# Rebuilding the convolution part of an S4 + MLP kernel: factored kernel tables in four channel chunks and a shifted 2048-point transform

## The chip, the cores and the metric

One core of one Trainium2 chip. The metric is the device time of one execution in microseconds. A *span* is the part of an execution that the profile covers; it is about 2 us shorter than the time.

Names of engines in the profile: PE is the TensorE matmul, PEld its weight load, DVE is VectorE, ACT is ScalarE, POOL is GpSimd, SP is SyncE (here it only issues DMA). `L88` is line 88 of the kernel that the line belongs to.

## The reference, cut to what matters

```python
def _A_ref(u, A_re, A_im, B_re, B_im, C_re, C_im, log_dt, Dskip):   # S4 convolution
    dt = exp(log_dt)[:, None]                    # D = 512 channels, N = 128 modes, L = 2048
    logdA = dt * (A_re + 1j * A_im)
    l = arange(L).astype(A_re.dtype)             # bfloat16: the time index is ROUNDED
    P = exp(logdA[:, :, None] * l)
    K = einsum("dn,dnl,dn->dl", C, P, dt * B).real
    y = irfft(rfft(pad(u)) * rfft(pad(K)))[:L]   # linear convolution by a 4096-point FFT
    return y + u * Dskip

h   = x + _A_ref(layernorm(x), ...)
out = h + mlp(layernorm(layernorm(h)))           # 512 -> 1376 -> 512, gelu
```

Two facts matter. The kernel `K` needs exponentials of 128 modes at 2048 times for 512 channels, which is done by products of small tables and a sum over modes on PE. And the time index is cast to bfloat16, which has 8 significant bits, so above 256 most indices coincide.

## The kernel before: the parts that matter

The tables of decay and phase are made for 256 channels at a time, twice. A table has 64 columns on one side (`P0`, 33 to -31) and 32 on the other (`Q1`, itself 4 x 8 products). POOL makes the arguments, ACT the exponentials and sines, DVE the products. POOL uses `tensor_scalar`:

```python
def trig_batch(nc, sc, pc, c2, js, halfpi):                 # 256 channels, 4 indices at a time
    for jj, j in enumerate(js):
        nc.gpsimd.tensor_scalar(Y[:, jj, :], psi_c, float(j), MAGIC, ALU.mult, ALU.add)
    nc.gpsimd.tensor_scalar(Q[:, :J, :], Y[:, :J, :], 1.0, -MAGIC, ALU.mult, ALU.add)
    for jj, j in enumerate(js):
        nc.vector.scalar_tensor_tensor(F[:, jj, :], psi_c, float(j), Q[:, jj, :], ALU.mult, ALU.subtract)
    ...                                                     # ACT: |F|, sin, cos
# exp_batch: nc.gpsimd.tensor_scalar(TH[:, jj, :], th_c, float(j), 0.0, ALU.mult, ALU.add), then ACT exp

for c2 in range(2):                                         # two halves of the channels, in turn
    tabs = gen_tables(nc, tb, sc, q1p, pc, c2, halfpi)
    kgen_matmuls(nc, kps_pool, tabs, c2, K_old)             # sum over modes: 512 small matmuls
k_to_tl(nc, tc, K_old, K_sb, identb)                        # permute
```

Then the transform of `K` goes through DRAM once, and the frequency loop takes 33 frequencies, with PSUM operands on DVE:

```python
for f1 in order:                                            # phase_u_main
    nc.tensor.matmul(X[:],  lhsT=Tall[:, f1, 64:192], rhs=B_all[:, f1, :], ...)
    nc.tensor.matmul(Xs[:], lhsT=Tall[:, f1, 0:128],  rhs=B_all[:, f1, :], ...)
    nc.vector.tensor_tensor(P1[:], X[:],  KF[:, f1, :], ALU.mult)
    nc.vector.tensor_tensor(P2[:], Xs[:], KF[:, f1, :], ALU.mult)
    ...                                                     # two matmuls to zp, ACT copies it to Z_sb
```

After it, Z goes to DRAM and comes back transposed (`ZT`), and the MLP follows, with `y2` on ACT in one block and a 16 us POOL addition of the bias b2.

## Time and profile before

| | us |
|---|---|
| time, median (four runs) | 587.77 (587.32 to 588.07) |
| start to first generation matmul | 159.9 |
| from there to ZT landed | 298.9 |
| ZT landed to the end of the span | 126 |

The page of the kernel before; first the busy time of each engine, then the busy tenths of 40 equal slices of the span (so one digit is 14.6 us):

```profile
span 584.6 us, 5246 instructions
PE 222.6 (38%) x1777; PEld 113.1 (19%) x1789; DVE 371.1 (63%) x600; ACT 249.9 (43%) x298; POOL 232.5 (40%) x259
...
PE   2004300000087000003966063299400501999997
DVE  6789897599969959996358166499508562200222
POOL 2930159887780899553782245400000000900000
```

No engine is full over the span, but PE has long rows of zeros where DVE and POOL read mostly 7 to 9 (5 at the least): PE waits for tables. The windows view of the kernel before gives the same by stage (columns: stretch, length, busy time and number of instructions of each engine, granted PE clock, DMA share, GB/s):

```profile
core 0: us, PE busy (x) PEld busy (x) DVE busy (x) ACT busy (x) POOL busy (x), PEclk, DMA share, GB/s
85.00:160.00 75.00, 0.10 (x4) 0.13 (x7) 63.36 (x88) 43.79 (x43) 62.99 (x89) 1.00 0.02 6
160.00:296.00 136.00, 47.72 (x1024) 46.83 (x1024) 104.18 (x140) 71.82 (x56) 87.34 (x77) 0.69 0.00 1
376.00:418.00 42.00, 38.28 (x125) 10.68 (x128) 39.74 (x66) 19.31 (x34) 0.62 (x1) 0.94 0.19 79
418.00:459.00 41.00, 0.00 (x0) 0.02 (x1) 13.12 (x2) 0.00 (x0) 1.84 (x3) 0.51 0.94 235
```

The groups of the page (line, engine, operation, out<-in, shape, count; then busy us and mean ns; then the idle time before them and what ended most of it) name the wait, 181.5 us of it, and the two instructions that fill POOL and DVE:

```profile
L198 PE MATMUL kps<-P0r,Q1r 128*32 128x64 bf16 x512 | 47.4, 389 | 184.7 <-DVE P0r L186 181.5
L86 POOL TENSOR_SCALAR TH<-th 128x256 f32<-128x256 f32 x86 | 66.2, 773 | 25.6 <-ACT P0r L91 10.8
L103 DVE SCALAR_TENSOR_TENSOR F<-psi,Q 128x256 f32<-128x256 f32 x86 | 50.5, 633 | 20.2 <-POOL Q L100 20.2
```

The chain of waits of the kernel before shows the 41 us in which only DMA runs (columns: start, length, what):

```profile
417.68 11.60 DMA Z_dram<-Z_sb
...
430.29 25.57 DMA ZT<-Z_dram
...
455.88 2.89 DMA ZT<-Z_dram
```

### The profile page before, as it was taken

Reading aid. Unit: us, or ns where it says so; the run is one execution under the profiler, and the core shown is the slowest. Engines: PE = TensorE matmul, PEld = TensorE weight load, DVE = VectorE, ACT = ScalarE, POOL = GpSimd, SP = SyncE. Lnnn points to the kernel's source line nnn. Section 1 sums busy time; section 2 is a strip of 40 time slices with the busy share of each in tenths; the row PEclk is TensorE's granted clock in tenths of the full one; section 3 lists DMA queues with packets and bytes.
Section 4 is the critical chain, followed back from the end, with each engine's and each line's share of the span. In section 5 each row is a group of like instructions: output and inputs, shape, how many; then the busy total and the mean of one; then the engine's idle time right before and its main releaser. Section 6 shows DMA issues by size and latency. Waiting matters only on the chain. (4 is left out here: it accounts for less than half of the span.)

```text
span 584.6 us, 5246 instructions
## 1 busy us (share of the span) xinstructions
PE 222.6 (38%) x1777; PEld 113.1 (19%) x1789; DVE 371.1 (63%) x600; ACT 249.9 (43%) x298; POOL 232.5 (40%) x259
## 2 busy tenths in 40 slices
PE   2004300000087000003966063299400501999997
PEld 1000000000086000003931010022100100544443
DVE  6789897599969959996358166499508562200222
ACT  3345335746699543463147141344200007777100
POOL 2930159887780899553782245400000000900000
PEclk9999999999999555555975567599855655899999
DMA  2412890000000000000071990021599170000122
GB/s 63 108 40 108 330 286 0 0 0 0 0 3 1 1 0 0 0 0 1 3 284 77 311 205 0 0 82 72 163 319 230 21 203 1 0 1 0 38 55 54
DMA packets 23307, 44.72 MB, mean 76 GB/s; under 512 B 6848, under 2 KB 19648, under 8 KB 21104
## 3 DMA queue, kind: packets, MB, share of 16 engines
q1 hardware_dynamic: 13408, 23.27, 13.0%
q10 hardware_dynamic: 8112, 12.10, 7.5%
q0 software_dynamic: 1760, 9.01, 4.7%
q8 instruction: 14, 0.23, 0.2%
q14 instruction: 13, 0.11, 0.1%
HBM read 27.40 MB, written 21.23 MB: 83 GB/s over the span
## 5 line engine op out<-in xcount | busy, mean ns | idle before, releaser
L198 PE MATMUL kps<-P0r,Q1r 128*32 128x64 bf16 x512 | 47.4, 389 | 184.7 <-DVE P0r L186 181.5
L86 POOL TENSOR_SCALAR TH<-th 128x256 f32<-128x256 f32 x86 | 66.2, 773 | 25.6 <-ACT P0r L91 10.8
L198 PEld LDWEIGHTS <-Q1r 128*32 128x32 bf16 x512 | 36.4, 179 | 182.3 <-issue 96.9
L103 DVE SCALAR_TENSOR_TENSOR F<-psi,Q 128x256 f32<-128x256 f32 x86 | 50.5, 633 | 20.2 <-POOL Q L100 20.2
L105 ACT ACTIVATE AF<-F 128x1024 f32<-128x1024 f32 (+1 forms) x22 | 30.6, 1390 | 58.6 <-DVE F L103 58.6
L98 POOL TENSOR_SCALAR Y<-psi 128x256 f32<-128x256 f32 x86 | 51.3, 601 | 5.3 <-ACT P0r L91 0.3
L532 DVE TENSOR_TENSOR ot<-o2ps,h_sb 128x512 bf16<-128x512 f32 x16 | 11.1, 691 | 63.9 <-PE o2ps L530 61.8
L199 PE MATMUL kps<-P0i,nQ1i 128*32 128x64 bf16 x512 | 47.3, 385 | 0.0
L100 POOL TENSOR_SCALAR Q<-Y 128x1024 f32<-128x1024 f32 (+1 forms) x22 | 34.5, 1568 | 17.0 <-DVE F L103 16.1
L523 PE MATMUL h1ps<-y2T,w_sb 128*128 128x512 bf16 (+1 forms) x171 | 40.5, 379 | 0.6 <-ACT hT L525 0.3
L530 PE MATMUL o2ps<-w_sb,hT 128*128 128x512 bf16 (+1 forms) x173 | 38.2, 379 | 0.2
L199 PEld LDWEIGHTS <-nQ1i 128*32 128x32 bf16 x512 | 36.7, 181 | 3.7 <-issue 3.7
L510 POOL TENSOR_TENSOR h_sb<-h_sb,b_b 128x8192 f32<-128x8192 f32 x1 | 15.7, 15727 | 49.4 <-ACT y_3293 L509 49.4
L525 ACT ACTIVATE hT<-h1ps,b_sb 128x512 bf16<-128x512 f32 (+1 forms) x44 | 30.1, 688 | 8.8 <-PE h1ps L523 8.8
L108 ACT ACTIVATE S<-F 128x1024 bf16<-128x1024 f32 (+1 forms) x22 | 30.7, 1394 | 0.1
L445 ACT CAST Z_sb<-zps 128x512 bf16<-128x512 f32 x33 | 19.2, 586 | 22.4 <-PE zps L444 22.4
L376 PE MATMUL u_aps<-u_sb,BD_108 64*128 64x512 bf16 x32 | 10.8, 590 | 45.1 <-DVE u_sb L421 40.8
L109 ACT ACTIVATE C<-AF,halfpi 128x1024 bf16<-128x1024 f32 (+1 forms) x22 | 26.3, 1194 | 0.0
L89 ACT ACTIVATE P0r<-TH 128x1024 bf16<-128x1024 f32 (+1 forms) x16 | 16.4, 1025 | 20.6 <-POOL TH L86 20.5
L406 ACT ACT_TABLE_LOAD x2 | 2.6, 1283 | 51.4 <-DVE h_sb L483 51.4
L482 PE MATMUL yps<-ZT,Dmat 128*64 128x512 bf16 x32 | 7.4, 514 | 43.2 <-DMA ZT<-Z_dram 42.0
L364 DVE CAST KF<-kfps 128x512 bf16<-128x512 f32 x17 | 11.0, 685 | 17.5 <-PE kfps L396 17.4
(346 smaller groups left out, 662.4 us busy)
## 6 DMA issues: line engine op xcount, KB each, us to landing
B_all<-Bt_dram SPq DMA_DIRECT2D x1, 4224.0 KB, 13.7
H_dram<-u_sb POOLq DMA_DIRECT2D x1, 2048.0 KB, 6.8
A_dram<-u_A SPq DMA_DIRECT2D x2, 1024.0 KB, 5.6
AK_dram<-k_A SPq DMA_DIRECT2D x2, 1024.0 KB, 4.8
Z_dram<-Z_sb SPq DMA_DIRECT2D x2, 1024.0 KB, 7.7
u_sb_3146<-H_dram SPq DMA_DIRECT2D x1, 2048.0 KB, 19.8
Bt_dram<-A_dram SPq DMA_DIRECT2D x6, 256.0 KB, 10.6
KF<-AK_dram SPq DMA_DIRECT2D x6, 256.0 KB, 12.8
```

The source lines that it names most:

```text
L86: nc.gpsimd.tensor_scalar(TH[:, jj, :], th_c, float(j), 0.0, ALU.mult, ALU.add)
L98: nc.gpsimd.tensor_scalar(Y[:, jj, :], psi_c, float(j), MAGIC, ALU.mult, ALU.add)
L100: nc.gpsimd.tensor_scalar(Q[:, :J, :], Y[:, :J, :], 1.0, -MAGIC, ALU.mult, ALU.add)
L103: nc.vector.scalar_tensor_tensor(F[:, jj, :], psi_c, float(j), Q[:, jj, :], ALU.mult, ALU.subtract)
L105: nc.scalar.activation(AF[:, :J, :], F[:, :J, :], ACT.Abs)
L108: nc.scalar.activation(S[:, :J, :], F[:, :J, :], ACT.Sin, scale=S2PI)
L109: nc.scalar.activation(C[:, :J, :], AF[:, :J, :], ACT.Sin, scale=-S2PI, bias=halfpi[:])
L198: nc.tensor.matmul(o, lhsT=Q1r[:, :, cc], rhs=P0r[:, :, cc], start=True, stop=False, tile_position=(0, 32 * g))
L199: nc.tensor.matmul(o, lhsT=nQ1i[:, :, cc], rhs=P0i[:, :, cc], start=False, stop=True, tile_position=(0, 32 * g))
L523: nc.tensor.matmul(pt[:fs, :], lhsT=w1_sb[:, dc, fc * P:fc * P + fs], rhs=y2T[:, dc, 4 * tb:4 * tb + 4, :], start=(dc == 0), stop=(dc == 3))
L525: nc.scalar.activation(hT[:fs, fc, 512 * tb:512 * tb + 512], pt[:fs, :], ACT.Gelu_apprx_tanh, bias=b1_sb[:fs, fc:fc + 1], scale=1.0)
L530: nc.tensor.matmul(pt[:], lhsT=hT[:fs, fc, j * P:(j + 1) * P], rhs=w2_sb[:fs, fc, :], start=(fc == 0), stop=(fc == NFC - 1))
```

## The change

Its intent is to do less table work and to overlap it.

- The bfloat16 rounding is used: the 2048 times have only 20 x 33 distinct parts that need a table. The factor C·B goes into the small table as a magnitude `G` and an angle `gam`, so there are no products to build it. 96 planes and 28 products become 53 planes.
- Phases are 32-bit integers, where a left shift does the wrap-around, in place of adding and subtracting a large constant.
- A 4096-point transform with 33 frequency groups becomes a quarter-shifted 2048-point one with 32, whose spectra are kept in bfloat16 in SBUF. A product then is one DVE instruction of 1024 columns. The second product needs the spectrum with its halves exchanged (`KFs`), which is made by DMA.
- The filter's work runs in four chunks of 128 channels; chunk c+1's tables are meant to fill the gaps of chunk c.
- In the tail, `y2` is pipelined on DVE by tile and b2 is a 97th row of w2.

The diff, cut to its core (constants, loads, and the `u` side are left out):

```diff
-JB = 4
-def trig_batch(...):            # 256 columns, POOL: mult+add
-        nc.gpsimd.tensor_scalar(Y[:, jj, :], psi_c, float(j), MAGIC, ALU.mult, ALU.add)
+def gen_tables(nc, tb, sc, pc, ch, halfpi):        # 128 columns, POOL: mult alone
+    for k0, n in [(1, 8), (9, 8)]:
+        for e in range(n):
+            gp.tensor_scalar(TH[:, e, :], thc, float(8 * (k0 + e)), None, ALU.mult)             # L287
+        act.activation(Br[:, 16 + k0:16 + k0 + n, :], TH[:, :n, :], ACT.Exp)
+        act.activation(Br[:, neg(k0, n), :], TH[:, :n, :], ACT.Exp, scale=-1.0)
+    for a0, n in [(0, 7), (7, 7), (14, 6)]:
+        for e in range(n):
+            gp.tensor_scalar(TH[:, e, :], thc, float(lA[a0 + e]), None, ALU.mult)               # L293
+        ...
+    for k0, n in [(1, 8), (9, 8)]:
+        for e in range(n):
+            gp.tensor_scalar(cod[:, e, :], psic, float(8 * (k0 + e) * 2 ** 24), None, ALU.mult) # L307
+        v.tensor_scalar(cod[:, :n, :], cod[:, :n, :], 8, None, ALU.logical_shift_left)          # L308
+        C, S = trig(cod, n, 1.0)
+        ...                                         # four DVE products; the same for Ar, Ai (L318 to L323)
+    for ch in range(4):
+        tabs = gen_tables(nc, tb, sc, pc, ch, halfpi)
+        kgen(nc, kpss, ch, tabs, Kg, ev)            # "generation": 256 small matmuls (L338, L339)
+        k_stage1(nc, mm, W, Kg, AK, ev)             # 128 small matmuls (L366)
+        nc.sync.dma_start(AK_dram[ch][:], AK[:])
+        for q in range(4):                          # read back transposed: pieces of 256 bytes
+            dqs[q % 2].dma_start(KF[32 * q:32 * q + 32], AK_dram[ch][32 * q:32 * q + 32].rearrange("f s d -> s f d"))
+        ...                                         # 32 matmuls, evicted to KF (L470)
+        nc.sync.dma_start(KFs[0:64], KF[64:128])    # L473
+        nc.scalar.dma_start(KFs[64:128], KF[0:64])
+        for f8 in range(0, 32, 8):
+            v.tensor_tensor(KF[:, f8:f8 + 8, :], KF[:, f8:f8 + 8, :], X[:, f8:f8 + 8, cs], ALU.mult)
+            v.tensor_tensor(KFs[:, f8:f8 + 8, :], KFs[:, f8:f8 + 8, :], X[:, f8:f8 + 8, cs], ALU.mult)
+            ...                                     # 16 matmuls, evicted to Z (L482, L483)
+        nc.sync.dma_start(Z_dram[ch][:], Z[:])
+    tables.close()                                  # only now is there room for w1, w2, b1, h, ZT
+    ...                                             # loads of w1, w2, b1 (2-byte pieces); L505 casts b1 on DVE
+    for ch in range(4):
+        for q in range(4):
+            dqs[q % 2].dma_start(ZT[32 * q:32 * q + 32, :, CW * ch:CW * ch + CW], Z_dram[ch]...)  # L511
```

The names in a chunk: `Kg` is the generated kernel, `AK` its first transform stage, `KF` its spectrum (made by the "filter matmuls", L470), `Z` the product with the spectrum of `u` after the inverse stage, `ZT` the same read back transposed.

## The prediction

> **What bounds it now.** No engine is full (page: DVE 371 of 585 us, ACT 250, POOL 233, PE 223); stages run in turn.
> - To 160 us: constants, layer norm, u transform, tables of 256 channels. From 85 to 160 (windows) DVE and POOL are busy 63 us each; in the waits the generation matmuls wait 181.5 us for DVE's table products.
> - 160 to 296: generation, second tables (208-290: DVE 62 us), generation.
> - 296 to 376: permute, FFT stage 1, DRAM round trip (PE idle 15.6 us), TP tables.
> - 376 to 418: frequency loop, DVE 95% busy on 66 PSUM products of 0.68 us.
> - 418 to 459: Z to DRAM and back alone: the chain has 11.6+25.6+2.9 us.
> - 459 to 585: h, layer norm (9.0 us for the b2 load), y2 on ACT (11.4 us), MLP 84 us.
>
> **Removed, added, moved.** Tables fall from 96 planes x 512 channels, plus 28 products, to 53 planes. POOL goes from about 205 us in table stages to 208 instructions of 128 columns, by estimate 60 us (256 columns took 399 ns at best), so DVE escapes contention (its 256-column F: 360 ns at best, 609 median). Permute and Xs matmuls go; 66 products become 32 bf16 ones of 1024 (0.60-0.68 us). But each of four chunks has a chain: generation (256 matmuls at 45 ns, 12 us), 128 small stage-1 matmuls, eviction, DRAM write and read-back in 256-byte pieces, 32 matmuls, half-swap DMA, products, 64 matmuls, Z write. Table work fills the gaps only partly: in program order DVE's last products of chunk c+1 stand behind the KF evictions of chunk c, so generation c+1 waits for chunk c's DRAM trip.
>
> **Sum (estimates from those durations).**
> - Start to first generation: DVE about 11 +20 (phase of C·B, W) +19 (T codes, statistics) +26 (u, evictions, skip) +5 TP +27 tables +10 X evictions = 118, plus waits 18: 137 us (160 before).
> - Chunk period: 48, 53, 53 us: generation, Z and stage 1 about 28, eviction 2, write 6, read 9, KF 6, rest waits. Generation of chunk 3 starts at 291.
> - Its drain is exposed: 28+2+6+9+10 (KF, half-swap) +13 (products, Z) +13 (Z write, last ZT quarter) = 81, plus 20 because w1, w2, h and three ZT quarters (8 MB) are issued just then. ZT complete near 392.
> - Tail 116 us instead of 126: y2 pipelined, no b2 wait.
>
> Together about 508 profiled. Some contention may hide: **500 us**, range **455 to 545**. Faster by over 2% 0.95, within 2% 0.03, slower 0.02.
>
> The Trainium skill, "DMA: Bandwidth & Descriptors" (Specifications), puts line rate at 512 bytes and more; the read-backs go from 1024 to 256 bytes. Before loaded 128 KB in such pieces in 2.3-3.0 us. "ScalarE: Activation LUTs" gives 1283 ns per table load; before shows that, 16 times; after has 21.
>
> **Right or wrong.** Right if first generation starts at 120-155 us; four periods of 45-60 us with DVE idle before the Kg and KF evictions; POOL under 90 us, DVE near 300; last ZT to end 110-120; TensorE waits for KF from DRAM in every chunk. Wrong if POOL still paces tables or PE is busy throughout.
>
> **What would make it wrong.** 256-byte reads far slower than 9 us per MB (+10 us per chunk makes 540); int32 shifts or reciprocal on DVE slow; half clock on PE (granted in 190-370); or better overlap, DVE-bound chunks of 40 us, giving 455.

## The result, and the profile after

Ratios here and below are the mean time of one kernel's fast runs over that of the other's of the same rounds, so they are not quite the ratios of the medians quoted.

| | before | after | predicted |
|---|---|---|---|
| time, median us (four runs each) | 587.77 | 479.03 (477.30 to 479.82) | 500 (455 to 545) |
| ratio, 95% interval | | 0.8148 (0.8129 to 0.8166) | |
| span, us | 584.6 | 477.8 | "about 508 profiled" |
| start to first generation | 159.9 | 134.4 | 137 |
| first to last generation | | 146.1 (49.9 + 48.9 + 47.3) | 154 (48 + 53 + 53) |
| last generation to ZT landed | | 85.4 | 101 |
| first generation to ZT landed | 298.9 | 231.5 | 255 |
| ZT landed to end | 126 | 112 | 116 |

The gain of 107 us in the span is thus 25.5 at the start, 67.4 in the middle and 14 in the tail.

The same parts of the page, of the kernel after (one digit is 11.9 us):

```profile
span 477.8 us, 6704 instructions
PE 203.9 (43%) x2576; PEld 128.4 (27%) x2584; DVE 263.4 (55%) x550; ACT 207.3 (43%) x257; POOL 135.2 (28%) x292
...
PE   2000033501641306630673056401252549999996
DVE  7289999980931765777487746210352983021022
POOL 5991740000399239923984000000010000000000
```

DVE lost 108 us and POOL 97. From the twelfth to the twenty-fourth digit (134 to 281 us) PE, DVE and POOL alternate: each chunk is visible as one bump. The windows of the kernel after, for the first wait, the chunk loop up to the last generation, the drain (from the last generation until ZT has landed) and the tail (columns as before):

```profile
85.00:134.00 49.00, 15.76 (x162) 9.05 (x160) 34.70 (x68) 25.20 (x39) 6.87 (x11) 0.72 0.63 150
134.00:281.00 147.00, 56.41 (x1404) 49.23 (x1408) 94.25 (x179) 93.44 (x109) 82.74 (x150) 0.58 0.31 73
281.00:366.00 85.00, 26.17 (x531) 23.17 (x520) 23.82 (x36) 11.07 (x17) 1.84 (x2) 0.60 0.83 182
366.00:478.00 112.00, 92.63 (x440) 42.61 (x448) 40.84 (x90) 31.73 (x33) 0.00 (x0) 0.86 0.08 19
```

In the loop no engine is busy for more than about 94 of 147 us, so no single engine bounds it; that a serial chain does is argued here and tested by e5_notab below. The granted PE clock in it is 0.58; what that adds to the chain was not tested. The groups show what POOL does (64 + 80 + 64 = 208 instructions, 121.9 us together, where the prediction had 60):

```profile
L287 POOL TENSOR_SCALAR TH<-th 128x128 f32<-128x128 f32 x64 | 38.4, 600 | 99.0 <-ACT S L301 90.2
L293 POOL TENSOR_SCALAR TH<-th 128x128 f32<-128x128 f32 x80 | 45.3, 594 | 3.0 <-ACT Br L289 1.8
L307 POOL TENSOR_SCALAR codb<-psi 128x128 int32<-128x128 f32 x64 | 38.2, 597 | 10.9 <-ACT Ar L294 4.2
```

They have half the columns of the ones in the kernel before, and take nearly as long. The view of waits of the kernel after names who waits (columns: engine, line, releaser; total us, number, longest):

```profile
DVE codb L308 <- POOL codb L307: 19.1, 5, 10.0
PE kfps L470 <- DMA KF<-AK_dram_62: 17.5, 1, 17.5
DVE b_sb L505 <- DMA b_bf<-in_B_b_dram: 11.7, 1, 11.7
ACT AK L86 <- DMA w_sb<-in_B_w_dram: 10.0, 1, 10.0
```

PE waits for KF from DRAM in each chunk (17.5, 17.4, 19.6 and 27.4 us). And the chain of waits of the kernel after, at the start of the last generation (`kps`), shows the predicted order: DVE's last table products (`Ai`, `Ar`) stand between and behind the KF evictions of the chunk before, and PE starts generation just after the last of them:

```profile
277.62 0.69 DVE KF L88
278.31 0.47 DVE Ai L322
278.77 0.58 DVE KF L88
...
279.93 0.56 DVE Ar L323
280.54 0.27 PE kps_90 L338 x4
```

Then the drain, in the same chain:

```profile
300.27 13.64 DMA b_bf<-in_B_b_dram
...
315.41 8.05 DMA AK_dram_65<-AK
...
323.93 9.08 DMA KF<-AK_dram_65
...
337.64 7.15 DMA KFs<-KF
...
353.46 4.26 DMA Z_dram_69<-Z
...
358.12 7.75 DMA ZT<-Z_dram_69
```

Stage 1 is done at 305.9, but its evictions are held by two loads that the engines reach first in program order: DVE casts b1 when its 2-byte pieces have landed (313.9), and ACT's queue waits for w2 (to 312.0). These two waits are called the walls below. The write of AK starts at 315.4 and takes 8.05 us, where those of the other chunks took 3.8 to 3.9.

### The profile page after: what moved, and what is told of

The parts are those of the page before. It is cut to its first block, busy times and chain, and to the rows that moved or that the text cites. A ratio compares the mean times of both kernels' runs of the same rounds, so it can differ in the third digit from the quotient of the medians.

```text
span 477.8 us, 6704 instructions
## 1 busy us (share of the span) xinstructions
PE 203.9 (43%) x2576; PEld 128.4 (27%) x2584; DVE 263.4 (55%) x550; ACT 207.3 (43%) x257; POOL 135.2 (28%) x292
## 5 line engine op out<-in xcount | busy, mean ns | idle before, releaser
L287 POOL TENSOR_SCALAR TH<-th 128x128 f32<-128x128 f32 x64 | 38.4, 600 | 99.0 <-ACT S L301 90.2
L470 PE MATMUL kfps<-KF,T 128*128 128x128 bf16 x128 | 14.3, 310 | 81.9 <-DMA KF<-AK_dram_65 27.4
L293 POOL TENSOR_SCALAR TH<-th 128x128 f32<-128x128 f32 x80 | 45.3, 594 | 3.0 <-ACT Br L289 1.8
L559 DVE TENSOR_TENSOR ot<-o2ps,h_sb 128x512 bf16<-128x512 f32 x16 | 11.1, 692 | 61.2 <-PE o2ps L557 42.6
L307 POOL TENSOR_SCALAR codb<-psi 128x128 int32<-128x128 f32 x64 | 38.2, 597 | 10.9 <-ACT Ar L294 4.2
L551 ACT ACTIVATE hT<-h1ps,b_sb 128x1024 bf16<-128x1024 f32 (+1 forms) x22 | 24.5, 1114 | 31.0 <-PE h1ps L549 30.9
L470 PEld LDWEIGHTS <-T 128*128 128x128 bf16 x128 | 13.3, 146 | 83.7 <-issue 83.7
L366 PE MATMUL k1ps<-Kg,W 20*128 20x256 bf16 (+1 forms) x512 | 23.1, 325 | 24.1 <-DVE AK L88 12.0
L482 PE MATMUL zps<-KF,TP_94 128*128 128x128 bf16 x128 | 24.9, 285 | 16.4 <-DVE KF L477 16.4
L366 PEld LDWEIGHTS <-W 20*128 20x128 bf16 x512 | 17.7, 117 | 28.0 <-issue 23.4
L483 PE MATMUL zps<-KFs,TP_95 128*128 128x128 bf16 x128 | 23.3, 282 | 2.7 <-DVE KFs L478 2.6
L557 PEld LDWEIGHTS <-hT 128*128 128x128 bf16 (+1 forms) x176 | 17.2, 98 | 20.8
L549 PEld LDWEIGHTS <-w_sb 128*128 128x128 bf16 (+1 forms) x176 | 17.5, 101 | 18.8 <-issue 0.2
L482 PEld LDWEIGHTS <-TP_94 128*128 128x128 bf16 x128 | 15.9, 131 | 20.9 <-DVE KF L477 16.5
L302 ACT ACTIVATE C<-AB,halfpi 128x1024 bf16<-128x1024 f32 (+2 forms) x20 | 21.1, 1055 | 0.3 <-ACT S L301 0.3
## 6 DMA issues: line engine op xcount, KB each, us to landing
X<-AU_dram ACTq DMA_DIRECT2D x2, 1024.0 KB, 19.6
```

The lines of the kernel that those rows point to most:

```text
L287: gp.tensor_scalar(TH[:, e, :], thc, float(8 * (k0 + e)), None, ALU.mult)
L293: gp.tensor_scalar(TH[:, e, :], thc, float(lA[a0 + e]), None, ALU.mult)
L302: act.activation(C[:, :n, :], AB[:, :n, :], ACT.Sin, scale=-SINSC, bias=halfpi[:])
L307: gp.tensor_scalar(cod[:, e, :], psic, float(8 * (k0 + e) * 2 ** 24), None, ALU.mult)
L366: nc.tensor.matmul(o, lhsT=W[rows, v, tl, :], rhs=r, start=(n == 0), stop=(n == len(js) - 1), tile_position=(32 * g, 0))
L470: nc.tensor.matmul(pt[:, k, :], lhsT=T[:, f0 + k, :], rhs=KF[:, f0 + k, :], start=True, stop=True)
```

## The experiments

The theory (A in most expectations): the sum of the prediction was right in its terms, and what is left to gain lies in two waits that the trace of the kernel after shows, POOL's slow table instructions and the two walls in the drain, so that taking each away gives about its length. The main rival (B): behind each wait lies another of nearly the same length, a serial chain in the loop and contention for DMA in the drain, so that taking one away moves the time little.

Twelve kernels ran. Each was timed in rounds with the kernel before on the same chip, whose median stayed between 587.8 and 588.9. The rounds ran on three chips and the kernel after was not timed again in them, so a difference from it, or between runs of different rounds, holds such a difference of rounds too. Stage times are those of each run's own trace. An edit is against the kernel after unless it says otherwise.

### What did the removed table work and the tail cost before?

**b1_notab**, against the kernel before; the second set of tables is not built (wrong, relative error 0.047).

```diff
-                        tabs = gen_tables(nc, tb, sc, q1p, pc, c2, halfpi)
+                        if c2 == 0:
+                            tabs = gen_tables(nc, tb, sc, q1p, pc, c2, halfpi)
```

> The kernel before, wrong result on purpose: the second set of tables (256 channels) is not built, the first is used twice. In the trace of before the second generation starts about 103 us after the first ends. Theory A, this table work lies wholly on the path: 95 to 110 us less, 478 to 493 us. Theory B, something else fills that gap: less than 60 us.

Measured: 490.90 us (ratio 0.8333, 0.8315 to 0.8350), 98 us less, in the range of theory A. The second set lay on the chain with nearly its whole length: before, the change had 98 us to gain there alone.

**b2_tail**, against the kernel before; the changed tail's `y2` by tile on DVE, and b2 as a row of w2.

```diff
+        nc.scalar.dma_start(w2_sb[96:97, 10, :], b2.rearrange("(o d) -> o d", o=1))
-        for j in range(16):
-            nc.scalar.activation(y2[:, j, :], h_sb[:, j, :], ACT.Identity, bias=nmr[:, j:j + 1], scale=rstd[:, j:j + 1])
-        nc.gpsimd.tensor_tensor(h_sb[:], h_sb[:], b2_b[:].unsqueeze(1).to_broadcast([P, 16, 512]), ALU.add)
+            nc.vector.tensor_scalar(y2[:], h_sb[:, j, :], rstd[:, j:j + 1], nmr[:, j:j + 1], ALU.mult, ALU.add)
```

> The kernel before with one part of the change alone: the second normalisation is applied on DVE tile by tile ahead of each transpose instead of 16 ACT passes first, and b2 comes as a 97th row of the last w2 block instead of a POOL addition. The pass on ACT took 11.4 us on the chain. Theory A: 6 to 11 us less, 577 to 582 us. Theory B, the MLP matmuls already hide it: within 2 us.

Measured: 577.48 us (ratio 0.9806, 0.9780 to 0.9831, so about the 2% line), 11.4 us less, as in theory A. That is most of the 14 us that the tail gained; the first MLP matmul starts at about 490 in place of 500 us.

### What do the tables cost after the change?

**e5_notab**: tables for chunk 0 alone (wrong, relative error 0.057).

```diff
-        tabs = gen_tables(nc, tb, sc, pc, ch, halfpi)
+        if ch == 0:
+            tabs = gen_tables(nc, tb, sc, pc, ch, halfpi)
```

> Wrong result on purpose: tables are built for chunk 0 only and reused by chunks 1 to 3, so all other work, the DRAM trips included, stays. Theory A, the tables (POOL codes first, DVE products last) set most of the period of 48 us: periods fall to 25 to 35 us and the time by 45 to 75 us, 405 to 435 us. Theory B, the chain through DRAM sets the period whatever the tables cost: at most 20 us less.

Measured: 445.37 us (ratio 0.7559), 33.7 us less. Both ranges were missed. The four generations now run close behind one another (from 136.8; all but the last 80 of 1,024 matmuls by 181.4 us, those at 194 to 196), but the filter matmuls still start at 168.7, 212.7, 259.8 and 303.1, a period of 43 to 47 us against 47 to 57 of the kernel after. So most of a period is not tables. It is a chain in series: filter matmuls, eviction, half-swap DMA, products, Z matmuls, then stage 1 of the next chunk (PE takes it in program order behind Z), its eviction, AK to DRAM and back. The run has a flaw of its own: without tables the MLP loads are released at about 195 us and stretch this very chain. In its trace the second KF read took 13.4 us and the half-swap after it 10.3, and the load of b1 entered the chain for 5.1; in the kernel after such a read takes 7.4 and a swap about 7. The last two AK writes took 9.0 each, where the kernel after had 3.9 in mid-loop. From this trace, first filter matmul to next AK write is 23.7 us; with 4.0 us for the write and the 7.4 us that the read takes in the kernel after, an undisturbed chain is about 35 us, an estimate. The other 12 to 15 us of a period would then be waits for tables. Together with b1_notab it shows how the large gain came about: a second table set cost 98 us before, and three sets after cost 34 us.

### Is POOL's table work the wait that is left?

**e3_twoop**: the three POOL lines take the two-operation form that the kernel before had, with a second operation that does nothing.

```diff
-            gp.tensor_scalar(TH[:, e, :], thc, float(8 * (k0 + e)), None, ALU.mult)
+            gp.tensor_scalar(TH[:, e, :], thc, float(8 * (k0 + e)), 0.0, ALU.mult, ALU.add)
(the same for the two other lines)
```

> The 208 POOL multiplications of 128 columns took 527 ns at best, while the kernel before had 399 ns at best for 256 columns with a multiply and an add. Only the form is changed: multiply and add zero. Theory A, the form with one operation is the slow one: 128 columns take 200 to 300 ns, POOL busy falls from 135 to 70-85 us, and the time by 6 to 14 us, as DVE waited 19.1 us for POOL's codes. Theory B, a fixed cost per instruction or contention with DVE: POOL stays at 130 to 140 us, time unchanged.

Measured: 462.52 us (ratio 0.7879, 0.7858 to 0.7900), 16.5 us less than the kernel after, correct, and the best correct kernel. That is theory A, and slightly past its ranges (6 to 14 us, and POOL busy 70 to 85 us). The view by line shows it; first the kernel after, then e3 (columns: number, then ns min/median/max, first and last start, shape):

```profile
L287 POOL TENSOR_SCALAR TH<-th x64: 527/528/1219, 9.9 to 232.3; 128x128 f32<-128x128 f32 x64
```

```profile
L287 POOL TENSOR_SCALAR TH<-th x64: 297/298/833, 10.5 to 217.8; 128x128 f32<-128x128 f32 x64
```

Adding an operation makes the instruction faster, 528 to 298 ns (medians). At 298 ns each the 208 instructions would make 62 us, close to the prediction's 60; in e3's trace they are busy 77.0 us, as their mean is above the median (371 to 397 ns by line, the longest 833). POOL is busy 90.7 us in place of 135.2, next to the predicted "under 90". DVE's wait for the codes, 19.1 us in the kernel after, is now:

```profile
DVE codb L308 <- POOL codb L307: 6.0, 4, 2.0
```

Generations start at 133.2, 172.7, 221.9 and 265.9; the first period fell by 10.4 us, about the 10 us that DVE waited for POOL in chunk 0 of the kernel after while AK evictions stood behind it. By stage the span's 17.3 us are 1.2 at the start, 13.4 in the periods, 2.6 in the drain and 0.1 in the tail. Why the one-operation form is slow was not tested: no run varied anything but the second operation, so the cause inside POOL stays open.

### Does another program order free the loop?

**e6_pipe**: the back half of chunk c (filter matmuls, swap, products, Z) is emitted after stage 1 of chunk c+1, so that PE's stage 1 no longer stands behind Z.

```diff
-    for ch in range(NCH):
+    def front(ch):      # tables, generation, stage 1, AK to DRAM and back
+        ...
+        return KF
+    def back(ch, KF):   # filter matmuls, swap, products, Z
+        ...
+    for ch in range(NCH + 1):
+        if ch < NCH: KFq[ch] = front(ch)
+        if ch > 0:   back(ch - 1, KFq[ch - 1])
```

> Source order only: the second half of chunk c (KF matmuls to Z) is written after the tables, generation and stage 1 of chunk c+1, so that generation c+1 no longer stands behind chunk c's trip through DRAM. Theory A, the in-order trip sets the period of 48 to 50 us: periods near 40 us, PE's waits for KF nearly gone, 15 to 25 us less, 455 to 464 us. Theory B, the table work itself or POOL sets it: period 46 to 50, within 5 us of the changed kernel.

Measured: 500.40 us (ratio 0.8516), 21 us slower. Generations start at 136.7, 180.7, 244.9 and 309.6. DVE waits 46.7 us for POOL's codes in the loop in place of 19.1 overall, up to 17.7 us at one place (line below), with an eviction behind it that PE needs: the new order puts DVE's next tables ahead of evictions, and POOL is slow at them. Both theories missed.

```profile
DVE codb L308 <- POOL codb L307: 46.7, 6, 17.7
```

**e8_twoop_pipe**: e6 and e3 together.

> e3_twoop with the source order of e6_pipe. e6_pipe alone was 21 us slower: POOL's codes, 527 ns each, came 17.7 us late in front of DVE's evictions. Theory A, with POOL at 298 ns the order now pays: 10 to 25 us less than e3_twoop, 438 to 453 us. Theory B, the trip through DRAM was never what set the period, and the order only lengthens the drain: 463 us or more.

Measured: 465.26 us (ratio 0.7893), 35 us faster than e6 but no better than e3 (the intervals of the ratios overlap). Theory B has the number (463 us or more) and not the reason: the drain is 5.5 us shorter than e3's (77.3 us) and the three periods together 6.9 us longer (139.6). DVE's wait for codes is down to 18.3 us, so the slow POOL form was the cause of e6's loss; what remains is that DVE stands 36.6 us (four times, up to 11.6) ahead of products for the half-swap DMA, as it had in e6 (37.4 us). Generations: 133.1, 166.9, 219.5, 272.7. The wait moved from PE's stage 1 to the swap.

```profile
DVE codb L308 <- POOL codb L307: 18.3, 6, 7.6
DVE KF L480 <- DMA KFs<-KF: 36.6, 4, 11.6
```

**e10_twoop_swapmm**: e3, with the half-swap made by PE: 64 more matmuls with the halves of T exchanged, evicted straight to KFs, and no DMA.

```diff
+            pw = mm.tile([P, 4, CW], f32, name="kfsps", tag="mm")
+                for r in range(2):
+                    nc.tensor.matmul(pw[64 * r:64 * r + 64, k, :], lhsT=T[:, f0 + k, 64 - 64 * r:128 - 64 * r], rhs=KF[:, f0 + k, :], ..., tile_position=(0, 64 * r))
-        nc.sync.dma_start(KFs[0:64], KF[64:128])
-        nc.scalar.dma_start(KFs[64:128], KF[0:64])
```

> e3_twoop, and the half-swapped KF spectrum comes from 64 small matmuls with the two halves of T exchanged, evicted straight into KFs, instead of two SBUF-to-SBUF DMAs after the eviction. With no tables at all the period stayed near 45 us, so a serial chain sets it: KF matmuls, half-swap DMA (6.9-7.2 us on the chain of e3_twoop), products, Z, stage 1 of the next chunk, DRAM trip. Theory A, that chain: 3 to 6 us less per chunk net of the added matmuls and evictions, 12 to 24 us in all, 439 to 451 us. Theory B, generation in program order hides the DMA except in the last chunk: at most 7 us less.

Measured: 483.96 us (ratio 0.8228), 21 us slower than e3. Both missed. The filter phase of chunk 0 takes 13.1 us in place of 3.7, and PE is busy in all of it, at a granted clock of 0.50. It saves about 7 us of DMA wait and costs 9.4 us, and generation of the next chunk, which in e3 had run during the swap and ended at 178.3 us, now mostly comes after the filter phase and ends at 195.6.

**e11_all3**: e10 with the order of e6.

> e10_twoop_swapmm with the source order of e6_pipe as well (second half of chunk c after stage 1 of chunk c+1). In e8_twoop_pipe the periods were 34, 53 and 53 us, with DVE idle 9 to 12 us before the products, on the half-swap DMA, in the middle of the next tables. Theory A, chain by DMA: with the half-swap DMA gone nothing on DVE or PE waits for a DMA in mid-chunk, periods fall to 36 to 42 us, 10 to 25 us less than e10_twoop_swapmm. Theory B, DVE's work (tables, products and evictions, about 45 us a chunk) is the next limit: within 8 us of e10_twoop_swapmm.

Measured: 466.82 us (ratio 0.7934), again no better than e3 (4.3 us more). That is 17 us less than e10, in theory A's range, but the periods are 33.8, 54.9 and 55.5 us and not 36 to 42, so its reason missed; theory B missed. e3, e8 and e11 take away different waits of the trace and end within 5 us of each other, which suggests that the loop has several chains of nearly the same length; no run shows that directly.

### Do the 256-byte pieces cost much?

**e4_contig**: KF is read in plain order, in pieces of 8 KB (wrong, relative error 0.021).

```diff
-            dqs[q % 2].dma_start(KF[...], AK_dram[ch][32 * q:32 * q + 32].rearrange("f s d -> s f d"))
+            dqs[q % 2].dma_start(KF[...], AK_dram[ch][32 * q:32 * q + 32])
```

> Wrong result on purpose: the changed kernel with the filter read KF taken from AK in plain order, so in pieces of 8 KB instead of 256 bytes. Theory A (the small pieces are a real cost of cutting to 128 channels): the read's time on the chain falls from 7.4 to 9.1 us to about 4, in each of the four chunks, and as it lies on the serial chain, the total falls by 8 to 16 us from the changed kernel's 479.0, to 463 to 471 us. Theory B (the read is bound by latency and by other transfers, or its time is hidden behind the next tables): at most 4 us less, 475 us or more.

Measured: 474.62 us (ratio 0.8046), 4.4 us less by the medians and 6 by the ratios; between the two ranges, nearer to B. A quarter (256 KB) lands in 3.2 us on SP's queue and 5.2 on ACT's, against 4.7 and 6.4 (medians of the first three chunks), so small pieces cost 1.2 to 1.5 us and not the half of the read. The filter matmuls of the four chunks start 0.5, 0.9, 1.1 and 3.9 us earlier; this run's first generation started 1.9 us later (136.3), so from there it is 2.4, 2.8, 3.0 and 5.8 us. The saving thus shows in the first chunk and the last, while the second and third add only 0.4 and 0.2; that tables hide it there is likely, not shown.

### What do the walls and the company in the drain cost?

**e1_b1cast**: the cast of b1 goes from DVE to POOL.

```diff
-    v.tensor_copy(b1_sb[:], b1_bf[:])
+    nc.gpsimd.tensor_copy(b1_sb[:], b1_bf[:])
```

> Only the cast of the b1 bias moves from DVE to POOL. In the drain of the last chunk DVE stands 11.7 us before this cast and ACT stands 10.0 us before its own stage-1 evictions (for the w2 load), both until 312-314 us. Theory A, two walls in parallel: taking one away gives at most 3 us, about 476 us. Theory B, the DVE wait is what costs: about 11 us less, 468 us.

Measured: 477.77 us (475.02 to 481.44), ratio 0.8136 (0.8092 to 0.8179): no difference that shows, as theory A said. DVE's wall is gone, but ACT still waits 10.0 us for w2 with the other half of the evictions behind it. AK is written 33.9 us after the last generation starts, against 34.9. Two waits run in parallel and end within 2 us of each other, so removing one of them gives almost nothing.

**e2_poolissue**: e1, and the loads of w1, w2, b1, b2, h and the first three chunks' ZT are issued by POOL, so neither DVE nor ACT nor their queues stand behind them.

```diff
-    nc.sync.dma_start(w1_sb[:], ...)
+    nc.gpsimd.dma_start(w1_sb[:], ...)
(the same for w2, b1, b2, h, and for ZT where ch < 3)
```

> As e1_b1cast, and w1, w2, b1, b2, h and the first three quarters of ZT are issued from POOL, idle at that point, so no DMA issue stands in the streams of ACT and SP before the evictions and copies of the last chunk. The bytes are the same. Theory A, in-order waits at issue: 10 to 16 us less than the changed kernel, 463 to 469 us. Theory B, the extra 20 us are contention for bandwidth: at most 3 us less.

Measured: 485.55 us (ratio 0.8272), 6.5 us slower than the kernel after; theory A missed, and contention (theory B) did more than cancel the gain. The chain of waits of e2:

```profile
306.51 11.61 DMA AK_dram<-AK
...
318.53 22.80 DMA KF<-AK_dram
```

The write starts 9 us earlier, as intended, and then takes 11.6 us in place of 8.05, and the read 22.8 in place of 9.1: the transfers that matter share the 16 DMA engines with 8 MB that do not. The traces bear this out: during the read the DMA engines moved 156 GB/s in e2 and 153 in the kernel after, so the rate was the same, but 3.56 MB in place of 1.46 went by, of which KF is 1. The Trainium skill, "DMA: Bandwidth & Descriptors" (Rules for kernel authors), says that spreading DMAs over issuing engines does not help bandwidth because all use the same 16 engines; this run agrees. In the kernel after, the walls had held the write back until w1, w2 and h had landed (312.2 us), and SP and ACT issued the twelve ZT pieces spread over 298 to 338 us; in e2 POOL issued all twelve at 311 to 324, on top of the read. In that sense the old order had worked as a brake.

**e12_held**: e3, with b1 loaded in the first phase, the other loads issued by POOL, and those of h and of the first three chunks' ZT held until the last KF has landed, by a one-column copy that needs KF.

```diff
+        if ch == NCH - 1:
+            nc.gpsimd.tensor_copy(hold[:], KF[:, 0, 0:1])
+        if ch < NCH - 1:
+            nc.gpsimd.tensor_copy(ZT[:, 0, CW * ch:CW * ch + 1], hold[:])
-            dqs[q % 2].dma_start(ZT[...], Z_dram[ch]...)
+            (nc.gpsimd if ch < NCH - 1 else dqs[q % 2]).dma_start(ZT[...], Z_dram[ch]...)
(the same hold for h; w1, w2 from gpsimd; b1 load and cast with the first phase's loads)
```

> The POOL two-operation form as in e3, and in addition the drain between the last generation and the last transposed read is relieved: the bias b1 is loaded in the first phase, its cast and all reads of w1, w2, h and of the transposed Z of the first three chunks are issued by POOL, and those of h and Z are held back (by a one-column copy that needs the last chunk's spectrum) until the last chunk's filter read has landed. Theory A (in e3 the last chunk's write of AK and its read of KF are slow, 8.2 and 9.2 us, and start about 11 us late because DVE and ACT stand behind bulk loads; take both the walls and the company away): AK write about 4 us, KF read 7 to 8 us, written from about 287 us instead of 298, the last ZT lands at 333 to 339 instead of 349, total 447 to 453 us. Theory B (company only moves: the held 5 MB then slow the half-swap, the Z write and the last ZT read as much as was gained): ZT lands at 345 or later, total within 4 us of e3's 462.5, or slower.

Measured: 469.33 us (ratio 0.7955, 0.7921 to 0.7989), some 5 us slower than e3 by the ratios and 7 by the medians; the profiled run was the slowest of the four, at 471.65. Two things happened. First, a fault of the edit: the scheduler put b1's cast at the front of POOL's program, where POOL waited 8.0 us for the load in 2-byte pieces, so all came late (first generation at 143.5 us, not 133.2). Second, the drain itself, from last generation to ZT landed, took 82.6 us against 82.8 in e3. The chains of waits of e3, then of e12:

```profile
298.20 8.16 DMA AK_dram<-AK
...
306.83 9.15 DMA KF<-AK_dram
...
320.60 7.20 DMA KFs<-KF
...
336.16 4.23 DMA Z_dram<-Z
```

```profile
302.47 3.86 DMA AK_dram<-AK
...
306.74 8.12 DMA KF<-AK_dram
...
319.48 12.53 DMA KFs<-KF
...
340.65 10.03 DMA Z_dram<-Z
```

The write and the read are 5.3 us shorter and AK is written 6 us sooner after generation (26.1 us, not 32.3), but the swap and the Z write are 11.1 us longer. That is theory B: the company moved. The drain has to bring in about 8 MB for which memory is free only when the tables are closed. Whether fewer bytes there, or room made earlier, would gain was not tried.

## Why the prediction was right, and where it was not

The time, 479.03 us, lies in the range, and the direction was nearly sure. The sum was 30 us too long (508 against a span of 477.8), and lowering it to 500 "as some contention may hide" had no ground. Point by point:

1. **Tables were the bound, and their removal the gain.** Right. b1_notab puts 98 us on one table set before; e5_notab puts 34 us on three sets after. What the shorter transform gave by itself was not run. The start (137 predicted, 134.4 measured), the tail (116, 112) and the first period (48, 49.9) came out close; the start in part by luck, as DVE was busy 104.8 us of it and not 118, and idle 29.6 and not 18. Over the whole span DVE was busy 263.4 us, not "near 300".
2. **The chunk as a chain.** Right in kind. The trace has the wait for KF in each chunk, and the last table products behind the KF evictions just ahead of generation. e5_notab qualifies it: with no tables at all the period is still 43 to 47 us, in part by loads that this run lets in early, so the serial part is most of the period (about 35 us by estimate) and the table wait is the smaller one.
3. **POOL: "by estimate 60 us", measured 121.9.** This is the term that failed by most. The estimate divided the duration of a 256-column instruction, without a look at its form: the kernel before used two operations, the change uses one, and that form takes 527 ns at least on 128 columns where two take 297. The rest is that the shortest duration was taken for all: with the two-operation form the 208 still took 77.0 us. "POOL under 90 us" is thus wrong for this kernel, and with the fast form e3 comes near it (90.7) and e8 meets it (88.1). The form cost 16.5 us of time, so the prediction's own sign of being wrong, "POOL still paces tables", was there in part.
4. **Generation, "12 us"**, took 6.1, 5.4, 7.7 and 10.7 us: in the first two chunks about half, so 45 ns per matmul was too much; the last two hold gaps of 2.0 and 5.5 us.
5. **Periods, 154 predicted, 146.1 measured.** Terms 3 and 4 have opposite signs here. That the sum looked good is luck: with POOL nearly as fast as estimated (e3), the periods are 132.7, so the chain's own terms had been set 21 us too long.
6. **Drain, 101 predicted, 85.4 measured.** From generation to the end of stage 1 took 25.4 (28 predicted), products and Z 8.5 (13). The allowance of 20 us for the loads measured 15: 9.5 of walls (the evictions behind them included), 4.2 on the AK write (8.05 against 3.9), 1.7 on the KF read (9.1 against 7.4). In e1, e2 and e12 it was not removed by changing the issuer or the order, only moved.
7. **256-byte reads, 9 us per MB.** Right: 7.4 to 9.1 us on the chain. The Trainium skill, "DMA: Bandwidth & Descriptors" (Specifications), asks 512 bytes for line rate; the direction agrees, but e4_contig shows that the pieces cost only 1.2 to 1.5 us of a quarter's landing and 4.4 us in all.
8. **Table loads on ACT.** The Trainium skill, "ScalarE: Activation LUTs" (What ACT_TABLE_LOAD costs), has about 1283 ns; the traces show 1283 ns before, and 21 loads of 1.28 us after, as counted.
9. **DVE escapes contention.** The trace is in line with it: the code instruction that took F's place runs at 279 ns at least and 287 median on half the columns, where F had 360 and 609: the median now lies at the minimum. No run isolates the cause.
10. **"9.0 us for the b2 load"** was a misreading: the chain's entry is the load of b1, in 2-byte pieces, and DVE's cast of it. The change did not remove it; it is the 11.7 us DVE wait in the drain, where a second wait of 10.0 us runs beside it (e1: nothing gained).

## What to carry to other kernels

Before scaling a duration from a trace to another size, check that the new instruction has the same operations: here one operation less made it take 77% longer. When a loop is bound by a chain, cutting one link can just promote the next; after the one cut that gained 16.5 us, three more in the loop and one in the drain gained nothing. And transfers that engines stand behind in program order may be acting as a brake for others: before freeing them, find where their bytes are to go.

## What the Trainium skill lacked or had wrong

- "GPSIMD Engine Reference" (Elementwise — side-by-side cycle accounting) gives about 2.6 cycles per element for the two-input `tensor_tensor`, and less for simpler loops, but no time for a `tensor_scalar` by its number of operations. Here a POOL `tensor_scalar` on 128 x 128 float32 takes 527 ns at least with one operation and 297 with two (e3_twoop), and 399 ns with two on 128 x 256. No page was found that tells the forms apart.
- "DMA: Bandwidth & Descriptors" has the rule on shared engines but no figure for a transfer that matters among bulk loads. Here a 1 MB write took 3.9 us alone, 8.05 and 11.6 in company, and a 1 MB read in 256-byte pieces 7.4, 9.1 and 22.8.
- The same page's 512-byte line has no measured time for shorter pieces on the queues of SP and ACT of this chip; its section "Why small descriptors are slow (HBM only)" reckons 27% overhead for 256 bytes. Here 256 KB took 4.7 and 6.4 us in 256-byte pieces, 3.2 and 5.2 in 8 KB pieces.
- The same page tells that a non-contiguous last dimension makes one descriptor per element, but not what a small one costs: the load of 1280 bias values in 2-byte pieces took 13.7 us to land in the kernel after, beside bulk loads, and 9.4 in e12_held, beside the loads of the first phase; the 96 values issued just behind it took 13.6 and 8.4.
